# Linear attention and a highway layer: queries turned by VectorE, smaller products, pair stores, another order

## The chip, the cores and the metric

The kernel runs on one core of a Trainium2 chip. A core has five engines with a queue of instructions each: TensorE (PE in the profile; PEld are its weight loads), VectorE (DVE), ScalarE (ACT), GpSimd (POOL) and SyncE (SP), which here only issues DMAs. Sixteen DMA engines move data between HBM and SBUF. The metric is the device time of one execution, in microseconds, as the median of several runs: 118.83 us before the change (118.77 to 118.89 in three runs).

## The reference

Eight batches, eight heads, 576 tokens, 64 numbers a head. Attention without a score matrix, and behind it a highway layer with two 512x512 weights:

```
q_s = softmax of q over the 64 numbers of a token
k_s = softmax of k over the 576 tokens
kv  = k_s^T v                # 64x64 for each batch and head
x   = q_s kv                 # 4608 tokens of 512 numbers
H   = max(x w_h, 0)
T   = sigmoid(x w_t + b_t)
out = T H + (1 - T) x
```

Inputs and output are float32, 9.4 MB each for q, k, v and the output.

## The kernel before

The kernel is one long list of steps, ORDER, written out by hand; each engine takes its own steps in that order, and waits where a step needs another's result. A step's name tells its work and place: `kv_3_0` is batch 3, `mt_12_0` tile 12; a letter behind a colon picks the engine (A ScalarE, D VectorE, P GpSimd, F a whole step instead of halves).

Tokens are worked in 36 tiles of 128 rows: of each pair of batches four tiles come from the first, four from the second, and one holds the 64 last rows of both. Tiles 27 to 35 belong to batches 6 and 7.

For a batch, q, k and v are loaded with 64 partitions a head, two heads side by side (`load_kv` L183, `load_q` L199 to L206; batches 4 to 7 have another cut of q, in pieces of 1 KB and 256 B). ScalarE takes exp of k and q to float16 (`ek` L253, `eq` L298 to L307), `vc` (L259) casts v. `kv` (L269) multiplies keys and values in blocks of 64x64 with a column of ones behind v, which gives the sums; `kr` and `kn` (L281, L287) divide, into `kvb`, which holds two heads on a diagonal of blocks. TensorE transposes exp q (`qt` L319, L324) into PSUM, and VectorE or ScalarE copies it out (`qc` L333); batch 7 is turned by two DMA transposes instead (`qd` L340). `xu` (L361) is the product of queries and kv of a tile in four products of 130 columns, `rs` and `x` (L370, L376) divide by the sums of the queries.

Then the highway layer, per tile: four transposes of x (`xt` L384), copied out by `xe` (L391); a PSUM bank that is filled with the bias (`bw`: by ScalarE L399, or by a product L401), four products with w_t on top (`mt` L411), tanh (`th` L433, L435); four products with w_h (`mh` L419). The weights are prepared so that with w_h' = (w_h - 1)/2 the step `dd` (L439) gives d = max(x w_h', -x/2), `uu` u = (1 + tanh) d, and `oo` (L471) out = u + x. `uu` is either one VectorE operation that reads the gate from PSUM (L453) or, where ORDER says P, two GpSimd operations g and u (L450, L451). `st` (L479 to L491) stores.

PSUM has eight banks: two for gates (`ps_t`), two for w_h products (`ps_g`), two for kv and xu (`ps_x`, one buffer of two banks), one for turned queries, one for turned x. All loads and nearly all stores go through SP's one DMA queue, in ORDER's order. At the start, TensorE multiplies blanks (`fill` L167) until there is work; batches 0 and 1 and tiles 0, 4 and 5 are worked in halves.

Of the kernel before, what the change touches and what calls it, by code (L numbers as in the profile page):

```python
# [8 lines left out]
FP32 = mybir.dt.float32  # L9
FP16 = mybir.dt.float16  # L10
# [6 lines left out]
b_0 q_0_0 v_0_1 setupdve k_0_0 b_32 eq_0_0 bsplit setuppool fill_5 fill_8 bp v_0_0 bc qt_0_0 ek_0_1 v_0_3 ek_0_0 k_0_2  # L17
v_0_2 vc_0_3:A bw_1 vc_0_0 ek_0_2 vc_0_2 q_0_4 vc_0_1:D ek_0_3 bw_0 w_h_0 fill_8 qc_0_0 whd_1:P kv_0_0 eq_0_1 w_h_2
w_t_2 kr_0_0 whd_0:P whd_2:P w_t_0 k_1_2 v_1_2 q_1_0 k_1_0 v_1_0 fill_5 q_1_4 kn_0_0 q_2_0 k_2_0 eq_0_2 xu_0_0 v_2_0
q_3_0 rs_0_0 whc_0:A x_0_0 k_3_0 fill_4 v_3_0 kv_0_1 fill_3 kr_0_1 kn_0_1 xu_0_1 rs_0_1 xu_1_0 rs_1_0 qt_0_1 x_1_0  # L20
fill_6 whd_3:P qc_0_1 xt_1_0 xu_3_0 qt_0_2 qc_0_2:A xe_1_0:D fill_1 rs_3_0 x_3_0 x_0_1 xt_3_0 xu_2_0 rs_2_0 x_2_0
wtc_2:P whc_2:A mh_1_0 wtc_0:P vc_1_3 ek_1_3 ek_1_2 vc_1_0 xe_3_0:D mh_3_0 dd_1 xt_0_1 xt_0_0 mt_1_0 xe_0_0:D mh_0_0
xe_0_1 dd_3 xt_2_0 mh_0_1 mt_0_1 th_1_0 xe_2_0:D dd_0 vc_1_2:A kv_1_1 uu_1_0 oo_1_0 eq_1_0 mt_0_0 th_0_0 ek_1_0 ek_1_1
kr_1_1 bw_3 qt_1_0 vc_1_1:A kn_1_1 qc_1_0 mt_3_0 xu_5_1 uu_0_0 mh_2_0 th_3_0 bw_2 rs_5_1 x_5_1 dd_2 xu_4_1 kv_1_0
kr_1_0 eq_1_1 rs_4_1 xt_5_1 mt_2_0 th_2_0 kn_1_0 bw_5 xe_5_1:D x_4_1 xu_5_0 mt_5_1 qt_1_1 eq_1_2 rs_5_0 x_5_0 xt_5_0
xu_4_0 bw_4:A uu_3_0:P oo_3_0 xe_5_0:D mh_5_1 rs_4_0 x_4_0 mh_5_0 xt_4_1 qc_1_1:A xt_4_0 xe_4_1:D dd_5 eq_2_0 xe_4_0:D
v_4_0 mt_5_0 th_5_0 xu_6_0 qt_1_2 rs_6_0 qc_1_2 oo_0_0 mt_4_1 mh_4_1 mh_4_0 uu_2_0:P x_6_0 mt_4_0 eq_2_1 xt_6_0 xu_8_0
uu_5_0 bw_6:A xe_6_0:D qt_2_0 rs_8_0 x_8_0 mh_6_0 oo_5_0 th_4_0 xt_8_0 dd_4 uu_4_0 xu_7_0 mt_6_0 ek_2_0:F rs_7_0
vc_2_2:A bw_8 xe_8_0:D mt_8_0 x_7_0 th_6_0 xt_7_0 th_8_0 oo_2_0 vc_2_0 kv_2_0 oo_4_0 qc_2_0 q_4_0 bw_7:A qt_2_1
qc_2_1:A dd_6 uu_6_0:P oo_6_0 eq_3_0:F xe_7_0:D kr_2_0 kn_2_0 mh_8_0 xu_9_0 rs_9_0 x_9_0 mt_7_0 th_7_0 bw_9 dd_8  # L30
uu_8_0:P qt_2_2 qc_2_2:A xu_10_0 bw_10:A xt_9_0 xe_9_0:D rs_10_0 x_10_0 ek_3_0 mh_7_0 dd_7 ek_3_2 mh_9_0 xu_12_0 k_4_0
xt_10_0 k_5_0 rs_12_0 qt_3_0 xe_10_0:D x_12_0 mt_9_0 th_9_0 uu_7_0:P q_4_9 dd_9 xu_11_0 qc_3_0 vc_3_2:A xt_12_0
mt_10_0 rs_11_0 mh_10_0 x_11_0 v_5_0 q_5_0 vc_3_0 st_1_1 q_5_9 uu_9_0 dd_10 oo_7_0 kv_3_0 qt_3_1 th_10_0 oo_8_0 st_1_0
xe_12_0 bw_12:A mh_12_0 kr_3_0 qc_3_1:A kn_3_0 xu_14_0 rs_14_0 x_14_0 bw_11:A xt_11_0 xe_11_0 mt_12_0 th_12_0 qt_3_2
v_6_0 xt_14_0 oo_9_0 k_6_0 xu_13_0 q_6_0 xe_14_0 mh_11_0 dd_12 qc_3_2 mt_11_0 rs_13_0 eq_4_0:F th_11_0 uu_12_0
uu_10_0:P x_13_0 dd_11 xu_15_0 rs_15_0 vc_4_0 mh_14_0 x_15_0 st_5_1 dd_14 qt_4_0 oo_10_0 vc_4_2 xu_16_0 rs_16_0 x_16_0
xt_13_0 xe_13_0:D oo_12_0 bw_14:A bw_13:A ek_4_0:F st_3_0 mt_14_0 th_14_0 xu_17_0 rs_17_0 bw_15:A x_17_0 qc_4_0
xt_15_0 mt_13_0 kv_4_0 xe_15_0:D kr_4_0 uu_11_0:P oo_11_0 th_13_0 qt_4_1 uu_14_0:P st_3_1 mh_13_0 vc_5_2 xt_16_0
kn_4_0 mh_15_0 xe_16_0:D vc_5_0 xu_18_0 ek_5_0:F dd_13 xt_17_0 qc_4_1:A uu_13_0 xe_17_0:D dd_15 rs_18_0 oo_14_0
bw_16:A mt_15_0 mh_16_0 x_18_0 th_15_0 uu_15_0:P mt_16_0 dd_16 mh_17_0 oo_13_0 bw_17:A th_16_0 oo_15_0 kv_5_0 uu_16_0  # L40
kr_5_0 kn_5_0 oo_16_0 eq_4_2 dd_17 qt_4_2 xt_18_0 eq_5_0 mt_17_0 st_5_0 xe_18_0 xu_20_0 rs_20_0 mh_18_0 qc_4_2:A
bw_18:A q_7_0 th_17_0 mt_18_0 eq_5_1 bw_20:A uu_17_0:P x_20_0 xt_20_0 dd_18 vc_6_2 xe_20_0:D xu_21_0 th_18_0 rs_21_0
st_7_0 v_7_0 qt_5_1 qc_5_1:A mt_20_0 x_21_0 xt_21_0 uu_18_0 eq_5_2 xu_19_0 xe_21_0:D qt_5_0 rs_19_0 x_19_0 st_7_1
mh_20_0 qc_5_0 bw_21:A st_10_1 vc_6_0 mt_21_0 th_20_0 dd_20 ek_6_0:F xu_22_0 bw_19:A rs_22_0 x_22_0 qt_5_2 th_21_0
qc_5_2:A eq_6_0 mh_21_0 bw_22:A xt_19_0 xe_19_0:D kv_6_0 dd_21 kr_6_0 kn_6_0 xt_22_0 uu_20_0:P mh_19_0 mt_19_0
xe_22_0:D dd_19 oo_17_0 xu_23_0 rs_23_0 oo_20_0 oo_18_0 mt_22_0 eq_6_1 qt_6_0 th_19_0 x_23_0 xu_24_0 uu_19_0 th_22_0
xt_23_0 xe_23_0:D k_7_0 mh_22_0 rs_24_0 bw_23:A x_24_0 mt_23_0 qc_6_0 xu_25_0 rs_25_0 x_25_0 st_10_0 uu_21_0:P oo_19_0
# [10 lines left out]
mh_32_0 dd_33 th_33_0 uu_33_0 xu_35_0 bw_32:A rs_35_0 oo_33_0 xt_34_0 mt_32_0 bw_34:A xe_34_0:D mh_34_0 st_33_0 x_35_0  # L58
xt_35_0 mt_34_0 dd_32 th_32_0 bw_35_1 oo_30_0 st_16_0 st_30_0 uu_32_0 xe_35_0 oo_32_0 mh_35_0 th_34_0 bw_35_0 mt_35_0
th_35_0 mt_35_1 dd_34 uu_34_0 oo_34_0 dd_35 uu_35_0 st_32_0 th_35_1 uu_35_1 st_34_0 oo_35_0 st_35_0 oo_35_1:D  # L60
st_35_1:A
"""


# [469 lines left out]
```

## Time and profile before

| | |
|---|---|
| median of the runs | 118.83 us |
| span of the profiled execution | 116.9 us |
| what lies around the span, to the median | 1.9 us |
| instructions | 3424 |
| DMA packets, bytes | 24195, 40.58 MB |
| packets under 512 B, under 2 KB | 5362, 11762 |
| share of the 16 DMA engines taken by SP's queue | 96.9% |

How to read it: the busy line gives the time in which each engine worked and its share of the span; the slices cut the span in 40 equal parts of 2.9 us, a digit 9 is a slice that is busy for 90% or more. The chain that ended last is followed back from the last instruction. A group's line gives source line, engine, operation, output and inputs by name, shape, count, then busy time and mean duration, then the idle time ahead of it and who ended it. A line of the timeline begins with start and duration in microseconds.

### The profile page before, as it was taken

What the parts mean: (1) busy time and instruction counts of PE and PEld (TensorE: products, weight loads), DVE (VectorE), ACT (ScalarE), POOL (GpSimd) and SP (SyncE); (2) the same over time, 40 slices, a digit from 0 to 9 for tenths busy, and PEclk for the clock granted to TensorE, in tenths of its full rate; (3) what the DMA queues carried; (4) which work ended last, traced back from release to release, by engine and by line L of the source; (5) the groups of instructions that cost most, each with busy time, mean ns of one, the idle gap of its engine ahead of it and who ended that gap; (6) DMA issues with size and microseconds to landing.
All of it is one profiled execution on the core that took longest, in us unless ns stands there. A gap on an engine that the chain in (4) does not pass through costs nothing.

```text
span 116.9 us, 3424 instructions
## 1 busy us (share of the span) xinstructions
PE 109.5 (94%) x1351; PEld 61.6 (53%) x1351; DVE 93.3 (80%) x222; ACT 90.0 (77%) x132; POOL 89.1 (76%) x99
## 2 busy tenths in 40 slices
PE   5999987999999999999999999999999999999930
PEld 2354544545665656565665547566564555554520
DVE  5642587589799979979889798988989887899870
ACT  4356461897999999989999999998597998545520
POOL 5022237208996999999999999999989699999960
PEclk9999999999999999999999999999999999999998
DMA  2999999999999999999999999999999956992875
GB/s 42 399 392 377 408 398 385 375 377 379 393 391 397 383 391 393 358 375 387 357 376 360 387 392 363 390 381 383 399 398 217 302 204 270 397 404 115 315 295 179
DMA packets 24195, 40.58 MB, mean 347 GB/s; under 512 B 5362, under 2 KB 11762, under 8 KB 24180
## 3 DMA queue, kind: packets, MB, share of 16 engines
q1 hardware_dynamic: 24032, 40.24, 96.9%
q8 instruction: 10, 0.16, 0.6%
q10 hardware_dynamic: 148, 0.14, 0.4%
q14 instruction: 5, 0.04, 0.1%
HBM read 30.41 MB, written 9.44 MB: 341 GB/s over the span
## 4 chain that ended last, share of the span: by engine, by line
PE 67%; POOL 15%; issue 6%; DVE 5%; DMA 3%; SPq 1%; POOLq 0%; DVEq 0%
PE tps L411 18%; PE gps L419 16%; PE turned L167 9%; POOL o L471 7%; PE xu L361 6%; PE turned L384 5%; PE kv L269 5%; PE qps L324 4%; POOL u L451 4%; DMA out_dram<-o 3%; POOL g L450 2%; PE qps L319 2%; POOL v L259 2%; DVE x L376 2%; PE tps L401 1%
## 5 line engine op out<-in xcount | busy, mean ns | idle before, releaser
L471 POOL TENSOR_TENSOR o<-u,x 128x512 f32<-128x512 f16 (+1 forms) x36 | 40.6, 1143 | 1.6 <-DVE u L453 0.7
L411 PE MATMUL tps<-w16t,xT 128*128 128x512 f16 (+1 forms) x148 | 37.3, 373 | 0.0
L419 PE MATMUL gps<-w16h,xT 128*128 128x512 f16 x144 | 36.8, 379 | 0.5 <-DVE xT L391 0.5
L376 DVE TENSOR_TENSOR x<-xu,rs 128x512 f16<-128x512 f32 (+1 forms) x39 | 25.2, 649 | 2.4
L259 POOL CAST v<-v 128x1152 f16<-128x1152 f32 (+1 forms) x14 | 14.0, 1010 | 14.7 <-DMA v<-in_v_dram 13.7
L439 DVE SCALAR_TENSOR_TENSOR d<-x,gps 128x512 f16<-128x512 f16 x36 | 24.5, 680 | 0.3
L451 POOL TENSOR_TENSOR u<-g,d 128x512 f16<-128x512 f16 x17 | 19.7, 1158 | 1.7 <-DVE rs L370 0.4
L253 ACT ACTIVATE ek<-k 128x576 f16<-128x576 f32 (+2 forms) x15 | 17.9, 1225 | 3.0 <-DMA k<-in_k_dram 3.0
L419 PEld LDWEIGHTS <-xT 128*128 128x128 f16 x144 | 13.0, 98 | 12.3 <-DVE xT L391 1.8
L399 ACT COPY tps<-ball 128x512 f32<-128x512 f32 x28 | 16.6, 597 | 3.5 <-DVE u L453 3.2
L411 PEld LDWEIGHTS <-xT 128*128 128x128 f16 x148 | 13.2, 98 | 10.6 <-DVE xT L391 0.4
L361 PE MATMUL xu<-kvb,eq 128*128 128x130 f16 (+1 forms) x160 | 14.8, 224 | 0.2 <-DVE kvb L287 0.2
L384 PE MATMUL turned<-idh,x 128*128 128x128 f16 x144 | 14.2, 220 | 0.5 <-DVE x L376 0.5
L391 DVE COPY xT<-turned 128x512 f16<-128x512 f16 (+1 forms) x28 | 10.9, 391 | 4.2 <-PE turned L384 3.0
L435 ACT ACTIVATE tps<-tps 128x512 f32<-128x512 f32 (+1 forms) x20 | 11.2, 559 | 3.6 <-PE tps L411 3.3
L453 DVE SCALAR_TENSOR_TENSOR u<-tps,d 128x512 f16<-128x512 f32 (+1 forms) x19 | 12.7, 671 | 1.4 <-ACT tps L435 0.6
L361 PEld LDWEIGHTS <-eq 128*128 128x128 f16 (+1 forms) x160 | 10.0, 100 | 7.3 <-DVE x L376 2.5
L167 PE MATMUL turned<-blank 128*128 128x512 f16 x40 | 12.4, 458 | 1.5 <-POOL blank L149 1.3
L384 PEld LDWEIGHTS <-x 128*128 128x128 f16 x144 | 9.8, 98 | 6.0 <-DVE x L376 2.1
L307 ACT ACTIVATE qe<-q 128x1024 f16<-128x1024 f32 (+3 forms) x9 | 9.4, 1052 | 4.1 <-DMA q<-in_q_dram 4.1
L450 POOL TENSOR_SCALAR g<-th 128x512 f16<-128x512 f16 x17 | 10.6, 621 | 0.9 <-ACT th L433 0.9
L433 ACT ACTIVATE th<-tps 128x512 f16<-128x512 f32 x17 | 10.0, 594 | 0.9 <-PE tps L411 0.9
(48 smaller groups left out, 106.8 us busy)
## 6 DMA issues: line engine op xcount, KB each, us to landing
k<-in_k_dram SPq DMA_DIRECT2D x6, 1152.0 KB, 12.2
v<-in_v_dram SPq DMA_DIRECT2D x6, 1152.0 KB, 12.0
out_dram<-o SPq DMA_DIRECT2D x23, 256.0 KB, 4.0
q<-in_q_dram SPq DMA_DIRECT2D x10, 512.0 KB, 11.5
out_dram<-o SPq DMA_DIRECT2D x6, 512.0 KB, 3.8
k<-in_k_dram SPq DMA_DIRECT2D x4, 576.0 KB, 9.3
q<-in_q_dram SPq DMA_DIRECT2D x2, 1152.0 KB, 14.2
q<-in_q_dram SPq DMA_DIRECT2D x2, 640.0 KB, 10.5
```

What stands on the lines that cost most here:

```text
L167: nc.tensor.matmul(spare, blank[:, 0:P], blank, start=True, stop=True, skip_group_check=True)
L253: nc.scalar.activation(t[:, :, c:c + n].rearrange("p j c d -> p c j d"), T[f"k32{b}"][:, c:c + n].rearrange("p c (j d) -> p c j d", j=NJ), ...
L259: copy(v16[b % NV][:, c:c + n, :, 0:D], T[f"v32{b}"][:, c:c + n].rearrange("p c (j d) -> p c j d", j=NJ))
L361: nc.tensor.matmul(dst, turned_q(b, jp, n), kvb[b % NKV][:, hh, kk], start=True, stop=True, skip_group_check=True)
L376: nc.vector.tensor_mul(t[:, k0:k1], sums(i, k)[:, :, :, 0:64], T[f"rs{i}_{k}"][:, 0:k1 - k0].unsqueeze(3).to_broadcast([P, k1 - k0, 4, D]))
L384: nc.tensor.matmul(t[:, n], T[f"x{i}"][:, n0 + n % 2:n0 + 2 * P:2], idh, is_transpose=True, start=True, stop=True, skip_group_check=True)
L399: nc.scalar.copy(t[:, cs], ball[:, cs])
L411: nc.tensor.matmul(T[gate(i, k)][:, cs], T[f"xT{i}"][:, n], w16["t"][:, n, cs], start=False, stop=(n == parts[-1] and not first), skip_gro ...
L419: nc.tensor.matmul(t, T[f"xT{i}"][:, n], w16["h"][:, n], start=(first and n == parts[0]), stop=(n == parts[-1] and not (first and len(part ...
L439: nc.vector.scalar_tensor_tensor(t, T[f"x{i}"], -0.5, T[f"gps{i}"], op0=ALU.mult, op1=ALU.max)
L451: nc.gpsimd.tensor_mul(t, g, T[f"d{i}"])
L471: eng.tensor_add(t[:, cs], T[f"u{i}_{h}"][:, cs], T[f"x{i}"][:, cs])
```

## The change

Queries are loaded with 32 partitions a head, four heads side by side, in runs of 18 tokens (`load_q`). Their exponentials are turned by VectorE in blocks of 32x32 words of 32 bits, that is two float16 numbers at a time (`tr`), straight from SBUF to SBUF, in three pieces for a batch; `qt`, `qc` and `qd` are gone. Even and odd numbers of a head then lie two bytes apart, and so kv is computed in parts for even and for odd numbers: 64 rows, 32 columns of the output (`kv`, 144 products a batch). `xu` multiplies 32 rows by 65 columns with four heads in the four row parts of the array, each with a PSUM bank of its own, for two tiles at a time ("a group"; there are 20). `rs` and `x` work on a group at once. `ps_x` is now four banks, used by kv and xu in turn; gates and w_h products share three banks (`ps_g`).

`uu` is always two operations, g and u, and each of them, like o, is on VectorE or on GpSimd as ORDER says. Bias is copied by ScalarE in all tiles but the last. Nothing is halved at the start; only the last tile is. Stores are of two tiles, with 4 KB a row, but for five single ones. The weight casts are on VectorE but for one. Pools change their numbers of buffers, and ORDER is new altogether.

```diff
-    ps_t = pool("ps_t", 2, space=PS)
-    ps_g = pool("ps_g", 2, space=PS)
     ps_x = pool("ps_x", 1, space=PS)
-    ps_q = pool("ps_q", 1, space=PS)
+    ps_g = pool("ps_g", 3, space=PS)
     ps_xt = pool("ps_xt", 1, space=PS)
...
+    def load_q(e, b, j, n):
+        t = landing("q", b, ldq).rearrange("p (c f) -> p c f", c=2)
+        rows = q[b].rearrange("(c g) (p j) d -> (g p) c (j d)", g=4, p=NQ)
+        nc.sync.dma_start(t[:, :, j * D:(j + n) * D], rows[:, :, j * D:(j + n) * D])
...
+    def kv(e, b):
+        ps = T[f"kvps{b}"] = ps_x.tile([P, 4, DM], FP32, tag="xu", name=f"kv_{b}")
+        for turn in range(2):
+            for c in range(2):
+                for j in range(NJ):
+                    for g in range(4):
+                        h = 4 * c + g
+                        hh, i, m = h % 2, h // 2, (turn + h) % 2
+                        rows, cols = slice(64 * hh, 64 * hh + 64), slice(32 * g, 32 * g + 32)
+                        nc.tensor.matmul(
+                            ps[cols, m, 65 * c:65 * c + 65], T[f"ek{b}"][rows, j, i, m:D:2],
+                            v16[b % NV][rows, i, j, 0:65], start=(j == 0), stop=(j == NJ - 1),
+                            skip_group_check=True, tile_position=(64 * hh, 32 * g))
...
+    def tr(e, b, j, n):
+        t = once(f"et{b}", lambda: etp.tile([P, 2, NQ * NT, 2], FP16, tag="et", name=f"et_{b}"))
+        src = T[f"qe{b}"].rearrange("p c f -> p (c f)").bitcast(FP32).rearrange("p (c j d) -> p c j d", c=2, d=NQ)
+        dst = t.rearrange("p c n m -> p (c n m)").bitcast(FP32).rearrange("p (c n) -> p c n", c=2)
+        if n == 8:
+            dst = dst[:, :, NQ * j:NQ * j + 256].rearrange("p c (a t i) -> p c i a t", a=2, i=4)
+            src = src[:, :, j:j + n].rearrange("p c (i a) d -> p c i a d", a=2)
+        else:
+            dst = dst[:, :, NQ * j:].rearrange("p c (t i) -> p c i t", i=2)
+            src = src[:, :, j:j + n]
+        nc.vector.transpose(dst, src)
...
+    def xu(e, u):
+        bs, J, its = groups[u]
+        t = T[f"xu{u}"] = ps_x.tile([P, 4, DM], FP32, tag="xu", name=f"xu_{u}")
+        if len(bs) == 1:
+            for a in range(2):
+                for c in range(2):
+                    for m in range(2):
+                        for g in range(4):
+                            col = 65 * (2 * a + c)
+                            rows = slice(32 * g, 32 * g + 32)
+                            nc.tensor.matmul(
+                                t[:, g, col:col + 65], turned_q(bs[0], c, m, 256 * J + P * a, P)(rows),
+                                kvb[bs[0] % NKV][rows, m, c, 0:65], start=(m == 0), stop=(m == 1),
+                                skip_group_check=True, tile_position=(32 * g, 0))
+            return
...
+    def gg(e, i, h=0):
+        eng = nc.vector if e == "D" else nc.gpsimd
+        eng.tensor_scalar(t[:, cs], T[f"th{i}_{h}"][:, cs], 1.0, 1.0, op0=ALU.add, op1=ALU.mult)
+
+    def uu(e, i, h=0):
+        eng = nc.vector if e == "D" else nc.gpsimd
+        eng.tensor_mul(t[:, cs], T[f"g{i}_{h}"][:, cs], T[f"d{i}"][:, cs])
...
+    def st(e, u):
+        dst = rows_at(bs[0] * S + 8 * J, [[NT * DM, NQ], [2 * DM, 4], [1, 2 * DM]])
+        nc.sync.dma_start(dst, T[f"oo{u}"].rearrange("p a n -> p (a n)"))
```

The new order ends so:

```
... st_6 mh_25 dd_25 mh_24 xt_27 xe_27:D dd_24 oo_23_0:D eq_7_0_8
tr_7_0_8 xu_16 rs_16 k_7_0_4 x_16 th_25_0 gg_25_0:P ... ek_7_0_4 kv_7 th_27_0 gg_27_0:D ...
mt_35_0 th_35_0 dd_35 gg_35_0:D uu_35_0:D
oo_35_0:P mt_35_1 th_35_1 gg_35_1:D st1_35_0:A uu_35_1:D oo_35_1:D st1_35_1:A
```

More of the change, by code (lines that the diff above doesn't have):

```diff
@@ L22 @@
[L22 to L26, printed above, removed]
@@ L112 @@
     NKV, NV = 3, 2
[L113 removed]
+    kvb = [consts.tile([P, 2, 2, 66], FP16, name=f"kvb{i}") for i in range(NKV)]
     v16 = [consts.tile([P, 4, NJ, 66], FP16, name=f"v16_{i}") for i in range(NV)]
```

439 lines of the change are left out of this document (159 added, 280 removed).

## The prediction

> **What bounds the kernel now.** I read the page's busy line and its slices first, then the chain that ended last, then the groups with their shapes kept apart, the timeline around the last keys, and the stretches of ten microseconds.
>
> ```profile
> PE 109.5 (94%) x1351; PEld 61.6 (53%) x1351; DVE 93.3 (80%) x222; ACT 90.0 (77%) x132; POOL 89.1 (76%) x99
> ...
> PE   5999987999999999999999999999999999999930
> ...
> DMA  2999999999999999999999999999999956992875
> GB/s 42 399 392 377 408 398 385 375 377 379 393 391 397 383 391 393 358 375 387 357 376 360 387 392 363 390 381 383 399 398 217 302 204 270 397 404 115 315 295 179
> ...
> HBM read 30.41 MB, written 9.44 MB: 341 GB/s over the span
> ...
> PE 67%; POOL 15%; issue 6%; DVE 5%; DMA 3%; SPq 1%; POOLq 0%; DVEq 0%
> ```
>
> TensorE is full from about 20 us to 111 us, and the DMA engines are full at some 385 GB/s until about 87 us. Both matter: TensorE sets the pace now, but no kernel can work on keys that have not landed. The groups give the prices (count, busy us, mean ns):
>
> ```profile
> L439 DVE SCALAR_TENSOR_TENSOR d<-x,gps 128x512 f16<-128x512 f16 x36 | 24.5, 680 | 0.3
> L376 DVE TENSOR_TENSOR x<-xu,rs 128x512 f16<-128x512 f32 x33 | 22.8, 690 | 2.2
> ...
> L451 POOL TENSOR_TENSOR u<-g,d 128x512 f16<-128x512 f16 x17 | 19.7, 1158 | 1.7 <-DVE rs L370 0.4
> ...
> L391 DVE COPY xT<-turned 128x512 f16<-128x512 f16 x23 | 9.5, 413 | 2.7 <-PE turned L384 1.5 <-ACT tps L435 0.7
> ...
> L333 DVE COPY eq<-qps 128x1024 f16<-128x1024 f16 x8 | 5.5, 684 | 1.6 <-PE qps L324 1.6
> ...
> L376 DVE TENSOR_TENSOR x<-xu,rs 128x256 f16<-128x256 f32 x6 | 2.5, 423 | 0.2
> ```
>
> The timeline shows how the end hangs on the last batch: its keys become exponentials (L253) at 90.11, keys times values (L269) follows at 92.80, and the last product with the gate weights (L411) ends at 112.1.
>
> ```profile
> 90.11 2.12 ACT L253 ACTIVATE ek<-k 128x2304 f16<-128x2304 f32 x1
> ...
> 92.80 0.78 PE L269 MATMUL kv<-v,ek 64*64 64x65 f16 x72
> ...
> 111.05 1.04 PE L411 MATMUL tps<-w16t,xT 128*128 128x256 f16 x8
> ```
>
> Between 93.6 and 112.1 TensorE has 18.5 us, and the instructions behind that kv add up to 18.6 us: no idle time. From 112.1 to the end are 4.8 us of tanh, u, o and the last store.
>
> **The change, part by part.** I work against the profiled execution: span 116.9 us; the median of 118.83 lies 1.9 us above it, added at the end. TensorE prices are those of the chain of waits: 0.86 us for four 512-column products, 0.22 for four transposes of x, 0.45 for eight of q, 0.23 for one tile's xu, 0.71 to 0.78 for a kv of 72.
>
> TensorE. Gone: 128 transposes of q (16 x 0.45 = 7.1), seven bias products (1.5). kv: 8 x 144 small products instead of 8 x 72. They are again 65 columns, four beside each other on different parts of the array, so I take the measured 0.75/72 = 10.4 ns each: 1.5 us a batch, 6 us more in all. xu: 640 products of 32 rows and 65 columns instead of 128 + 32 of 130 columns. Ends: 10.4 ns (the kv row) or, with no overlap, half of the 57 ns that one xu product of 130 columns takes, 28 ns; 6.7 to 18 us against 8.4 now. The kv row is the nearest (same columns, partial array): 6.7, and 11 us more at the other end. After a kv the chain has 0.55 instead of 0.45 for the next eight transposes, so 0.1 us for a switch; there are 28 such blocks instead of 14: 1.4 more. Sum: -7.1 - 1.5 + 6 - 1.7 + 1.4 = -3 us of some 95.
>
> ScalarE. Without the q copies (6 x 1.01 + 6 x 0.38) but with seven more bias copies (0.6 each), and the exponentials of q whole: 90.0 becomes about 89. GpSimd: 15 of the o additions leave (1.16 each), three g come (0.62): 89.1 becomes about 74.
>
> VectorE. Gone: the q copies (6.0), the fused u that read PSUM (19, 12.7), the half-array kvb products (20, 7.4; now 8 x 0.424 = 3.4). x and its reciprocal go in pairs: 1024 elements are 0.690 + 2 x 0.267 = 1.22 (0.267 from the 256- and 512-element rows), 16 x 1.22 + 4 x 0.69 = 22.3 against 25.3. Added: 15 o of the 512 form (0.69, as x): 10. The 32x32 transposes (16 of 512 words, 8 of 128) have no row: between 0.35 (the 512-element cast, L236) and 1.22 (if the strided writes cost double); I take 0.62, between twice the 256-word memset (0.272) and the 0.68 of 512-element operations: 11.5 in all. 17 g: 0.35 to 0.69, taken 0.38 (nearest: the cast and the xT copy, one 16-bit source): 6. 20 u: 0.41 to 0.69, taken 0.5: 10. Weight casts and subtractions from POOL and ACT: 3. The groups now add to 101.5 us of durations for 93.3 busy (back to back, operations overlap: x at 47.67, u at 48.28, d at 48.88), mine to about 112, so 103 busy: 10 more. At the low ends it would be 6 us less, at the high ends 16 more.
>
> The new u, g and o on VectorE read only SBUF, while GpSimd reads SBUF for its own u, g and o. In the trace of before VectorE's elementwise work always has one operand in PSUM, and GpSimd's o never strays from 1.156 us (0.667 is the half tile), so a collision is not seen there, nor excluded. The bounds for one are 0 and one GpSimd operation (1.16).
>
> [...]
>
> DMA. The reads stay; q now comes in runs of 4.6 KB instead of 1 KB and 256 B, and the two DMA transposes go. What counts is when the last keys land, since all is in one queue. Before, ten stores of 262 KB stand in front of them: 30.4 - 0.26 + 2.6 = 32.8 MB, at 384 GB/s from 2.9 us on, 88 us; ScalarE took them at 90.1 without waiting. After, seven pair stores and two single ones stand in front: 34.6 MB. At 389 GB/s (slices 2 to 13, without the small q pieces) that is 2.9 + 34.5/0.389 = 91.6, and 0.7 for the landing (0.524 MB of q should be through at 3.9 and was taken at 4.68): 92.3. With 400 throughout (slices with 4 KB weight rows show 398 to 408) it is 89.9; with 380, 94.4. These nine stores wait for o of old tiles, which are long done, and loads are issued some 12 us ahead, so SP's queue should not starve.
>
> The start: batch 0 is no longer halved, so kv 0 needs all keys and values (2.4 MB: 9.5 us) but q comes after. The last w_h block lands at about 18, its subtraction and cast on VectorE take 1.5; the first products start at 17 to 20, as now (18.1). Nothing gained or lost: from 25 us the next keys set the pace.
>
> Middle. Counted with the rows, each VectorE duration less the 0.08 that overlaps, VectorE has 15.7 us queued between kv 5 and kv 6, TensorE 14. By the same rate kv 5 can start at 69.0 (24.65 MB through at 66.0, 0.7 to land, two casts of 1.15), kv 6 at 81.9 (29.8 MB, 0.7, exponential 2.1): 12.9 us. From kv 6 to kv 7 there are 10.2 us of TensorE work for 12.4. At full speed kv 7 is 0.6 late. Also gates and values now share three PSUM banks instead of two and two, and kv and xu one set of four, so each kv or xu waits for a 1.2 us x; the wait "xu for x" is 2.5 us in 8 cases now. At 95% of full speed the two stretches take 27.3 for 25.3: 2 us late.
>
> The end. Keys 92.3, exponential 2.1, kv 1.5: 95.9. Behind it TensorE has 8 tiles: 15 groups of four at 0.86 and two half ones (0.9), six transposes (1.3), three xu (1.0), switches (0.4): 16.6. Then 4.85 as now, with g and u (0.8) in place of a 0.42 u partly beside other work. 95.9 + 16.6 + 4.85 = 117.3 without any stall. The late middle adds 2; VectorE has 16 us of work in the same 16.6, so I add 0.8 for waits (xu of the last group waits for a pair's x with 1.9 us of products to cover 2.4). 120.1; plus 1.9: **122.0 us**, slower by 2.7%. Undisturbed, 119.2; at 389 GB/s and 90% of full speed, 124.5.
>
> **The rivals.** *Faster.* The DMA runs at 400 GB/s with the longer runs: keys at 89.9, and both VectorE and TensorE keep their tail full. 89.9 + 2.1 + 1.5 + 16.6 + 4.85 + 1.9 = 116.9; it decides once keys land before 91.6 us and nothing stalls. For it: the kernel before has a tail without idle time. Against it: VectorE had 20% of slack there and has none here.
>
> *VectorE and GpSimd get in each other's way.* Some 53 VectorE operations read SBUF alone; GpSimd is busy 74 of 118 us (0.63), the rest of an operation is half of 1.16: 0.37 us each on average. 27 of the 53 stand in the two stretches where VectorE has no slack (8 after kv 5, 19 after kv 7): 10 us, of which I take 4 to fall into the slack before kv 7 or behind GpSimd's last work: 122 + 6 = 128 us. For it: nothing before put both engines on SBUF together. [...]
>
> *The small products don't overlap.* xu costs 28 ns: 0.56 us more for each of 20 groups; four groups after kv 5 and three after kv 7 are on the path: 122 + 4 = 126. Against it: the kv row.
>
> **How the numbers follow.** Forecast (119.3 to 124.5): 0.45. Collision (124.5 to 131): 0.27. Small products: 0.07. Faster: 0.17, and within 0.2%, which is about what a measurement of this kernel can tell from no change: 0.04. Range 117.0 to 128.8: it leaves out some of the faster cases and the upper half of the collisions, 2 in 10. Faster 0.17, same 0.04, slower 0.79.
>
> **What would show it.** kv 7 near 96 to 98 us with the exponential in front waiting for the DMA; VectorE at 100 busy us or more; xu at 0.33 us a pair in the chain; transposes near 0.62; tail of some 22 us from kv 7 on. It is wrong if VectorE's g, u and o run far longer than 0.38, 0.5 and 0.69 beside GpSimd, if small products do not overlap, or if the keys land before 91.6.

## The result, and the profile after

The changed kernel takes 145.87 us, 27.0 us more than the kernel before, which took 118.86 us beside it: a ratio of 1.2258, with a 95% interval of 1.222 to 1.2296. One of its four executions fell into a slower state and took 152.99 us; executions over 1.5% above the fastest of their kernel count in the median of 145.87, but in no ratio, and in no time of the experiments below, where the changed kernel stands at 145.7 us. The prediction was 122.0 us with a range of 117.0 to 128.8. Slower was right; the size was not, by 24 us, and none of the rivals reached so far: the collision with GpSimd, the dearest of them, was put at 131 us at most. The profiled execution took 145.68 us with a span of 143.6.

The page of the changed kernel, with the lines that answer to those of the kernel before, and the line of the queue that fetches instructions:

```profile
PE 109.4 (76%) x2266; PEld 56.9 (40%) x2266; DVE 114.4 (80%) x216; ACT 83.3 (58%) x112; POOL 76.3 (53%) x82
...
PE   6965097597697798578799745999985999799430
...
PEclk9999658999999999999999996899999999999997
DMA  4999999999999799996599940795991280813233
GB/s 144 355 385 411 399 391 389 391 399 402 388 403 375 246 376 409 379 395 266 167 349 383 383 159 6 230 407 201 304 306 62 112 335 0 322 48 146 108 145 114
...
q8 instruction: 17, 0.28, 0.8%
...
HBM read 30.41 MB, written 9.44 MB: 277 GB/s over the span
...
DVE 47%; PE 30%; issue 8%; DMA 7%; SPq 3%; POOL 1%; ACT 1%; DVEq 0%; POOLq 0%
```

TensorE's busy time is what it was (109.5 before), but spread over 27 us more, with 24 of the 40 slices under 90% (5 before), and twice within the kernel its clock falls. The DMA engines are no longer full: 277 GB/s for 341. VectorE has 21 us more work than before, and leads the chain. "issue", time for which the profile names no releaser, is 8% of a longer span. The costliest groups of VectorE, and its g, shapes kept apart:

```profile
L363 DVE SCALAR_TENSOR_TENSOR d<-x,gps 128x512 f16<-128x512 f16 x36 | 24.0, 676 | 2.0 <-PE gps L353 2.0
L320 DVE TENSOR_TENSOR x<-xu,rs 128x1024 f16<-128x1024 f32 x16 | 19.5, 1220 | 0.8
L279 DVE STREAM_TRANSPOSE et<-qe 128x512 f32<-128x512 f32 x16 | 17.5, 1103 | 4.8 <-ACT qe L261 4.8
L375 DVE TENSOR_TENSOR u<-g,d 128x512 f16<-128x512 f16 x18 | 12.1, 676 | 0.9
L387 DVE TENSOR_TENSOR o<-u,x 128x512 f32<-128x512 f16 x14 | 11.1, 796 | 0.8 <-POOL u L375 0.7
...
L369 DVE TENSOR_SCALAR g<-th 128x512 f16<-128x512 f16 x15 | 7.1, 474 | 0.0
```

What the new work costs is higher than I took it: the turn 1.10 us for 0.62, u 0.68 for 0.5, o 0.80 for 0.69, g 0.47 for 0.38. The x of a pair is 1.22, as forecast.

The end, from the timeline (start, duration): the last exponentials of keys, the last keys times values, the last gate product, the last o of VectorE.

```profile
113.18 2.12 ACT L223 ACTIVATE ek<-k 128x2304 f16<-128x2304 f32 x1
...
115.77 1.35 PE L244 MATMUL kv<-v,ek 64*32 64x65 f16 x144
...
136.70 1.03 PE L347 MATMUL tps<-w16t,xT 128*128 128x256 f16 x8
...
139.86 0.43 DVE L387 TENSOR_TENSOR o<-u,x 128x256 f32<-128x256 f16 x1
```

kv 7 starts at 115.8 instead of 92.8; from there to the end of the span it is 27.8 us instead of 24.1. So 23 of the 27 us are lost before the last batch.

**Where TensorE stops.** The timeline of TensorE around the second dip of its clock:

```profile
83.44 1.44 PE L244 MATMUL kv<-v,ek 64*32 64x65 f16 x137 [0.75 <-DVE x L320]
87.66 0.29 PE L244 MATMUL kv<-v,ek 64*32 64x65 f16 x7 [2.79 <-issue]
87.88 0.61 PE L327 MATMUL turned<-idh,x 128*128 128x128 f16 x4
88.28 1.91 PE L353 MATMUL gps<-w16h,xT 128*128 128x512 f16 x4
```

In the middle of one kv, 137 of 144 products done, TensorE stands still for 2.8 us though keys and values are there, and nothing on another engine ends the wait. Afterwards four products take 1.91 us instead of 1.03, and the granted clock is 0.50 from 87.31 to 90.72. A stop of 2.6 us of the same kind lies within an xu and ends at 61.85. The records of the instruction queue (16 KB blocks) show a block that comes in from 59.29 to 60.38 and one from 84.81 to 86.23; TensorE goes on 1.47 and 1.43 us after these. That was not in the prediction, and the experiments are mostly about it.

### The profile page after: what moved, and what is told of

Its sections match the earlier page's. It is cut to its first block, busy times and chain, and to the rows that moved or that the text cites. A ratio compares the mean times of both kernels' runs of the same rounds, so it can differ in the third digit from the quotient of the medians.

```text
span 143.6 us, 5179 instructions
## 1 busy us (share of the span) xinstructions
PE 109.4 (76%) x2266; PEld 56.9 (40%) x2266; DVE 114.4 (80%) x216; ACT 83.3 (58%) x112; POOL 76.3 (53%) x82
## 4 chain that ended last, share of the span: by engine, by line
DVE 47%; PE 30%; issue 8%; DMA 7%; SPq 3%; POOL 1%; ACT 1%; DVEq 0%; POOLq 0%
PE gps L353 11%; DVE x L320 8%; DVE d L363 7%; DMA q<-in_q_dram 7%; PE tps L347 6%; DVE o L387 6%; DVE et L279 6%; DVE u L375 6%; PE turned L327 4%; PE kv L244 4%; DVE xT L333 4%; DVE g L369 3%; PE xu L292 3%; SPq L169 2%; DVE w16h L199 2%
## 5 line engine op out<-in xcount | busy, mean ns | idle before, releaser
L359 ACT ACTIVATE th<-tps 128x512 f16<-128x512 f32 (+1 forms) x37 | 21.1, 580 | 27.2 <-PE tps L347 27.1
L387 POOL TENSOR_TENSOR o<-u,x 128x512 f32<-128x512 f16 (+1 forms) x22 | 25.1, 1139 | 19.4 <-DVE u L375 18.6
L279 DVE STREAM_TRANSPOSE et<-qe 128x512 f32<-128x512 f32 (+1 forms) x24 | 19.9, 834 | 4.8 <-ACT qe L261 4.8
L320 DVE TENSOR_TENSOR x<-xu,rs 128x1024 f16<-128x1024 f32 (+1 forms) x20 | 22.3, 1114 | 0.8
L261 ACT ACTIVATE qe<-q 128x1024 f16<-128x1024 f32 (+1 forms) x16 | 18.6, 1161 | 7.2 <-DVE et L279 4.4
L369 POOL TENSOR_SCALAR g<-th 128x512 f16<-128x512 f16 x20 | 14.2, 717 | 15.6 <-ACT th L359 15.6
L223 ACT ACTIVATE ek<-k 128x2304 f16<-128x2304 f32 (+1 forms) x10 | 17.3, 1735 | 4.0 <-DMA k<-in_k_dram 4.0
L244 PE MATMUL kv<-v,ek 64*32 64x65 f16 x1152 | 11.8, 192 | 5.6 <-issue 3.2
L375 DVE TENSOR_TENSOR u<-g,d 128x512 f16<-128x512 f16 (+1 forms) x20 | 13.0, 655 | 1.1
L244 PEld LDWEIGHTS <-ek 64*32 64x32 f16 x1152 | 10.4, 91 | 8.5 <-issue 5.0
L333 DVE COPY xT<-turned 128x512 f16<-128x512 f16 x27 | 11.0, 408 | 2.2 <-PE turned L327 2.0
```

What stands on the lines that cost most here:

```text
L244: nc.tensor.matmul(ps[cols, m, 65 * c:65 * c + 65], T[f"ek{b}"][rows, j, i, m:D:2], v16[b % NV][rows, i, j, 0:65], start=(j == 0), stop=(j ...
L261: nc.scalar.activation(t[:, :, j * D:(j + n) * D], src[:, :, j * D:(j + n) * D], AF.Exp)
L279: nc.vector.transpose(dst, src)
L320: nc.vector.tensor_mul(dst[:, :, 0:n], sums(u)[:, :, :, 0:64], T[f"rs{u}"][:, :, 0:n].unsqueeze(3).to_broadcast([P, 4, n, D]))
L359: nc.scalar.activation(t[:, cs], T[f"tps{i}_{h}"][:, cs], AF.Tanh, scale=0.5)
L375: eng.tensor_mul(t[:, cs], T[f"g{i}_{h}"][:, cs], T[f"d{i}"][:, cs])
```

## The experiments

Two theories. *VectorE*: its work, 93 to 114 us, and the lengthening beside GpSimd set the pace. *Instructions*: the 144 products of a kv, each with a weight load, use up TensorE's instructions faster than they arrive; it stops, and its clock falls. Either would leave the late transfers as a consequence. All times are medians beside the kernel before (118.8 to 119.0). Where the time rests on one execution, the text says "single": two executions of one of these kernels can lie 2 to 5 us apart, so that a single one decides only about more.

### One part at a time

**e1_plain_turn**: the turned blocks are written side by side (the rows of x then stand in another order).

```diff
-dst[:, :, NQ * j:NQ * j + 256].rearrange("p c (a t i) -> p c i a t", a=2, i=4)
+dst[:, :, NQ * j:NQ * j + 256].rearrange("p c (i a t) -> p c i a t", a=2, i=4)
```

> The 32x32 blocks are written next to each other instead of four words apart (the numbers of x land at other tokens; the amount of work is the same). Before the change a 512-element operation took 0.68 us; the turn of 512 words takes 1.10 us in the changed kernel. If the strided write doubles it, it falls to about 0.6, VectorE is 8 us shorter and the time falls by 6 to 9 us from 145.9. If a turn simply costs two cycles for each word, it stays at 1.10 and the time stays within 1 us.

149.5 us, single. The turn alone, from the groups of this run:

```profile
L279 DVE STREAM_TRANSPOSE et<-qe 128x512 f32<-128x512 f32 x16 | 11.0, 694 | 4.8 <-ACT qe L261 4.8
```

So 0.41 of the 1.10 us are the strided write, and without it the turn is near the 0.62 that I took. VectorE's busy time falls by 5.6 us, to 108.8, and the time does not fall, which neither expectation had. TensorE has three long stops for instructions here (2.06, 4.92 and 2.12 us) instead of two.

**e2_no_pool_gu**: GpSimd's g and u left out.

```diff
 def gg(e, i, h=0):
+    if e != "D":
+        T[f"g{i}_{h}"] = T[f"th{i}_{h}"]   # and u likewise: d
+        return
```

> All g and u that ORDER gives to GpSimd are left out (20 and 17 operations, 36 us of GpSimd; u then takes tanh or d in their place, so the output lacks these factors); those on VectorE stay. Theory of the collision: VectorE's g falls from a mean of 0.47 towards 0.28 and its u from 0.68 towards 0.42, the values that they have in the changed kernel when GpSimd rests; VectorE gets 5 to 8 us shorter and the time falls by 5 to 9 us. Rival, that these are the operations' own durations: means stay, and the time falls by less than 3 us, by the shorter way from tanh to o alone.

150.7 us, single. VectorE's g falls to 0.42, u to 0.62 in the eight that still read a g (0.50 in the ten others), o to 0.77, and its busy time by 2.5 us, less than the 5 to 8 expected. The time does not fall; the stops are 2.06, 5.63 and 2.73 us.

**e3_kv64**: kv in 72 products of 64x64, as before the change.

```diff
-ps[cols, m, 65 * c:65 * c + 65], T[f"ek{b}"][rows, j, i, m:D:2],
+ps[cols, hh, 65 * c:65 * c + 65], T[f"ek{b}"][rows, j, 2 * c + w],   # 64 columns
```

> Keys times values in 72 products of 64x64 a batch as before the change, instead of 144 of 64x32 (the blocks then lie where the queries don't look for them, so x is another one; reads, waits and the rest of the order stay). 1152 instructions fewer in TensorE's queue. Theory of the instruction supply: the blocks of instructions on the queue for them fall from 17 to about 12, the two waits of 2.6 and 2.8 us of TensorE that end with no other engine named go, and with 5 us less of products the time falls by 5 to 10 us. Rival, VectorE is full anyway: the gain becomes idle time of TensorE, and the time falls by less than 2 us.

141.38 us, single; VectorE leads the chain with 57%, its busy time is unchanged at 113.7, 13 instruction blocks come in instead of 17, and there is no stop over 1 us for instructions. A gain of 4.3 us, with TensorE 3 us less busy; it lies between the two expectations and within what two executions can differ by.

**e4_act_stores**: every store on ScalarE's queue.

```diff
-nc.sync.dma_start(dst, T[f"oo{u}"].rearrange("p a n -> p (a n)"))
+nc.scalar.dma_start(dst, T[f"oo{u}"].rearrange("p a n -> p (a n)"))
```

> All stores are issued by ScalarE's queue, at the same places of the order, so that loads behind them in SP's queue don't wait for them. In the changed kernel the keys of batch 7 are issued at 99.7 us, behind stores that wait for o. Theory of the queue: they are issued before 85 us, kv 7 comes 8 us earlier or more and the time falls by 5 to 10 us. Rival, that VectorE's and TensorE's work sets the pace and the late loads are only its consequence: the keys come earlier, kv 7 does not, and the time moves by less than 2 us, or up a little for the waits on ScalarE.

149.76 us, single; the keys of batch 7 leave at 73.0, but kv 7 starts at 117.9, no earlier. Nothing that I did to one part alone was worth more than 4.3 us, and what was to help VectorE helped nothing. Either of two causes could stand behind the other, so the next runs put each into the kernel before, alone.

### Each cause alone, in the kernel before

**e5_before_kv32** and **e9_before_kv32_look** (the same kernel): each 64x64 product becomes two of 64x32.

```diff
+for s in (0, 32):
-    nc.tensor.matmul(ps[cols, ...], T[f"ek{b}"][rows, j, 2 * kk + w], ...)
+    nc.tensor.matmul(ps[64 * w + s:64 * w + s + 32, ...], T[f"ek{b}"][rows, j, 2 * kk + w, s:s + 32], ...)
```

> The kernel before with one thing changed: each 64x64 product of keys times values is made of two products of 64x32 that write the same sums, 576 more pairs of TensorE instructions (about the number of the changed kernel), everything else as it was, VectorE's work too. Instruction supply as a cause of its own: waits of 2 us or more inside or right before kv that nothing on another engine ends, an instruction block landing where they end, a granted clock of 0.5 behind them, and 126 to 138 us. VectorE as the only cause: the dearer kv alone, 8 x 0.75 = 6 us on a TensorE that is 94% busy, no such waits, 123 to 125 us.

> The same kernel as e5_before_kv32 once more, for a profile that is not disturbed. Instruction supply: 142 to 146 us again; waits of 1 us or more on TensorE put down to nothing on another engine (issue) in or right before kv, each ending when a 16 KB instruction block lands, and stretches of granted clock 0.5 behind them; VectorE some 94 busy us as before. If kv itself is what takes the 25 us: keys times values of 3 us and more each without gaps, clock 1.0.

143.91 us (ratio 1.2096, 1.2061 to 1.2132), and 143.76 in e9, single: 25 us more, above the 126 to 138 of the first expectation, with VectorE's work unchanged at 93.7 busy us. One more execution of e5, the one that was profiled, took 228 us (so did one of the kernel before beside it, 224) and tells nothing of the time. TensorE's waits, its granted clock in 40 slices, and the timeline around the first stop, all of e9:

```profile
PE kv L270 <- issue: 10.0, 3, 5.0
PE gps L422 <- issue: 4.5, 1, 4.5
...
PEclk9999999999999998699975799996599999999998
```

```profile
49.81 1.21 PE L270 MATMUL kv<-v,ek 64*32 64x65 f16 x127
56.06 0.32 PE L270 MATMUL kv<-v,ek 64*32 64x65 f16 x17 [5.04 <-issue]
56.31 1.04 PE L327 MATMUL qps<-idh,qe 128*128 128x128 f16 x8
57.14 1.91 PE L422 MATMUL gps<-w16h,xT 128*128 128x512 f16 x4
```

Three stops of 5.04, 4.46 and 4.67 us, 14.2 in all, where the kernel before has none. With each the granted clock falls to 0.5, together for 17 us; 13.2 of them lie behind the stops, which at half speed are worth up to 6.6 us. A kv itself takes 1.35 to 1.47 us where no stop falls in it.

**e10_before_kv130**: the 72 products stay, each 130 columns wide.

```diff
-ps[cols, hh, 65 * kk:65 * kk + 65], ..., v16[b % NV][rows, 2 * kk + w, j, 0:65],
+ps[cols, hh, 130 * kk:130 * kk + 130], ..., v16[...][rows, ..., 0:65].unsqueeze(1).to_broadcast([64, 2, 65]),
```

> The kernel before with each of the 72 products of keys times values 130 columns wide instead of 65 (the values twice beside each other; the second half is not read): TensorE's time for keys times values doubles by about as much as in e5_before_kv32 (0.75 us a batch, 6 us in all), the number of instructions stays. If the number of instructions cost e5_before_kv32 its 25 us: 122 to 126 us, no waits for instructions, clock near 1.0. If it was TensorE's time or PSUM: 135 to 145 us, as e5_before_kv32.

122.34 us (1.0253 to 1.033), as expected if the number of instructions was the cause.

```profile
PE 113.1 (94%) x1351; PEld 64.9 (54%) x1351; DVE 93.5 (78%) x222; ACT 90.1 (75%) x132; POOL 88.9 (74%) x99
```

A kv of six batches takes 1.26 us for 0.78, so TensorE has nearly the extra work of e9 (there 1.35 to 1.47), no instruction more, no stop and no dip of the clock. It costs 3.5 us. The other 21 us of e9, less some 0.1 to 0.2 us a kv, come with the number of instructions; the stops and the half clock behind them, 14.2 and up to 6.6 us, account for nearly all of it.

**e16_before_turns**: two turns a batch on VectorE, written as the changed kernel writes them, into a tile that nothing reads.

```diff
 def kn(e, b, k):
+    for s in range(2):
+        nc.vector.transpose(aside.rearrange("p (c a t i) -> p c i a t", c=2, a=2, i=4), words_of_ek[512 * s ...])
```

> The kernel before with two turns of 512 words a batch added on VectorE behind the normalized keys times values, with the same strided writes as the changed kernel's, into a tile that nothing reads: 16 x 1.10 = 17.6 us more VectorE work, 111 of 117 us busy, no TensorE instruction more. The counterpart of e9_before_kv32_look. If VectorE's work alone can cost the old kernel its 27 us: 126 to 140 us. If VectorE's slack takes most of it: 119 to 124 us.

134.44 us (ratio 1.131, 1.1245 to 1.1376), within the 126 to 140 for VectorE's work alone.

```profile
L294 DVE STREAM_TRANSPOSE aside<-ek 128x512 f32<-128x512 f32 x16 | 17.8, 1114 | 1.7 <-ACT ek L253 1.2
```

17.8 us more VectorE work cost 15.6 us, although VectorE idled 24 of 117 us before. Its slack was not usable for these: they stand in pairs of 2.2 us behind a kv, ahead of the x and the copies of turned queries that TensorE waits for next. The place counts, then, as well as the amount. Either cause alone can therefore cost the old kernel a lot: the instructions 21 to 25 us, the turns put in this place 16.

### Both in the changed kernel

**e6_kv64_plain_turn**: e3 and e1 together.

> The changed kernel with keys times values as 72 products of 64x64 (as in e3_kv64, so sums land in other places) and with the turned blocks written side by side (as in e1_plain_turn; the rows of x then stand in another order). Compared with e3_kv64 (141.4 us) it differs by the turns alone, and there are no long instruction waits to hide what they are worth. If VectorE sets the time once instructions arrive: 16 turns are 0.41 us shorter each, 6.5 us of busy time, and most of it shows: 135 to 138 us, last keys times values before 109 us. If the time hangs on instruction supply or transfers: 140 to 142 us, as e3_kv64.

136.29 us (ratio 1.1434, 1.1351 to 1.1517), as expected if VectorE sets the time once instructions arrive. With 72 products the shorter turn is worth 5 us (against e3, single); with 144 (e1) it was worth nothing.

**e13_no_turn** and **e14_kv64_no_turn**: the turns of batches 1 to 7 left out, with 144 products and with 72.

```diff
 def tr(e, b, j, n):
+    if b > 0:
+        T[f"et{b}"] = T["et0"]
+        return
```

> The changed kernel with the turns of batches 1 to 7 left out (the query weights of batch 0 are used for all batches): VectorE is some 16 us less busy, TensorE's instructions are the 2266 pairs of the changed kernel. If instruction supply holds the changed kernel by itself: 142 to 151 us, no gain against 145.9. If VectorE's work sets the time: 128 to 134 us.

> e13_no_turn with keys times values as 72 products of 64x64: 1152 TensorE instructions fewer, the same VectorE work. Compared with e3_kv64 (141.4 us) it differs by the turns, compared with e13_no_turn by the instructions. If both causes hold, either hidden behind the other: 122 to 130 us, 10 us or more under e3_kv64 and 12 us or more under e13_no_turn. If VectorE's work is not a cause: 134 to 141 us, as e6_kv64_plain_turn and e11_kv64_plain_fused.

146.23 us (145.7 to 147.1) and 132.44 us (131.9 and 133.0). The busy lines, e13 and then e14:

```profile
PE 112.6 (78%) x2266; PEld 58.8 (41%) x2266; DVE 101.2 (70%) x195; ACT 83.1 (57%) x112; POOL 76.8 (53%) x82
```

```profile
PE 101.5 (78%) x1690; PEld 52.0 (40%) x1690; DVE 101.1 (78%) x195; ACT 82.6 (63%) x112; POOL 78.0 (60%) x82
```

With 13 us less VectorE work the 144 products hold the time where it was: four stops for instructions, 9.7 us for the 5.4 of the changed kernel, and a granted clock of 0.5 for 14 us in the middle. Only with 72 products does the work taken from VectorE show. e14 fell between its two expectations: 14 us under e13, but 9 us under e3 where 10 or more were expected. Without the turns xu no longer waits for the exponentials of its queries either, and that is in these two times.

**e11_kv64_plain_fused** and **e12_plain_fused**: VectorE's pairs of g and u are one operation on PSUM again, with 72 and with 144 products.

```diff
+nc.vector.scalar_tensor_tensor(u, T[f"tps{i}_{h}"], 1.0, T[f"d{i}"], op0=ALU.add, op1=ALU.mult)
-g = th + 1; u = g * d
```

> e6_kv64_plain_turn (136.5 us) with one step less than e8_kv64_plain_fused_back: where g and u are both VectorE's they are one operation on the tanh in PSUM again, while the casts and subtractions of the gate weights stay on VectorE. Some 5 us less busy on VectorE, which was 97 to 99% busy from 40 us on in e6_kv64_plain_turn. If VectorE sets the time there: 130 to 133.5 us, and the 139 us of e8_kv64_plain_fused_back come from its start. If VectorE's busy time does not matter: 136 to 139 us.

> e11_kv64_plain_fused with keys times values in 144 products of 64x32 as in the changed kernel, so the changed kernel with turned blocks side by side and with g and u fused on VectorE. VectorE is some 11 us less busy than in the changed kernel. If instruction supply is a bound of its own there: 141 to 149 us, hardly below the 145.9 of the changed kernel, waits for instructions of 2 us and more, and 8 us or more above e11_kv64_plain_fused. If VectorE alone sets the time: 132 to 137 us, within 4 us of e11_kv64_plain_fused.

137.75 us (1.1561 to 1.1646) and 150.06 us (1.2536 to 1.2711). In e11 the second expectation came true: VectorE is only 2 us less busy (107.1, for the 5 that I took) and the time rises a little. The gate stays in PSUM until the fused operation has read it, and the wait of ScalarE's next bias copy for VectorE's d, 9.3 us in e6, is 16.3 here. The gap between the two, 12.3 us, is the price of the 144 products once more: their stops, the half clock behind these, and some 5 us of TensorE's own work.

**e8_kv64_plain_fused_back**: e11, and the weight casts and subtractions back on GpSimd and ScalarE (six letters in ORDER, such as `wtc_2:D` to `wtc_2:P`).

> e6_kv64_plain_turn with VectorE's load taken down to about that of before: where g and u are both VectorE's they are one operation on the tanh in PSUM again, as before the change, and the casts and subtractions of the gate weights go back to GpSimd and ScalarE. VectorE overfull as the main cause of what is left: some 8 us less busy, the first product with the gate weights earlier than 24 us, 125 to 131 us. Something else (the order of the work, the wider exponentials, PSUM shared by kv, xu and x): VectorE's busy time falls, but the time stays at 133 us or more.

139.08 us (1.1636 to 1.1725); here too the second expectation came true: VectorE 102.5 busy, and no gain. Its busy time by itself is not the measure; at the start it only moves the wait (VectorE 3.5 of 10 us busy from 20 to 30 us, 7.8 in e6).

The square, in us; an asterisk marks a single execution:

```
                                  144 products   72 products   difference
turn as changed                      145.7          141.4*         4.3
turn side by side                    149.5*         136.3         13.2
turn side by side, g and u fused     150.1          137.8         12.3
no turns in batches 1 to 7           146.2          132.4         13.8
```

Down the left column nothing helps, down the right one the turns do. My reading: the instructions hold the left column near 146 or above, and in the changed kernel itself VectorE stands so close behind them that removing them alone shows 4.3 us. The square fits this; that the upper right corner is a single execution leaves the 4.3 uncertain by some us.

**e7_kv64_plain_no_pool_gu** and **e15_kv64_no_turn_no_pool_gu**: e6 and e14 without GpSimd's g and u.

> e6_kv64_plain_turn without GpSimd's g and u (left out: the steps behind them read the tanh and the difference instead). VectorE keeps every instruction. If VectorE loses time because its SBUF-only operations run beside GpSimd: g from about 0.47 to 0.35 us, u from 0.68 to 0.5, o a little shorter, some 5 us of VectorE's busy time, and 128 to 133 us (part of it because o no longer waits for GpSimd's u). If collisions are a side matter: VectorE's durations stay, and 134 to 138 us, within 1.5 us of e6_kv64_plain_turn.

> e14_kv64_no_turn without GpSimd's g and u. VectorE's instructions are the same, but fewer of them run beside GpSimd, and o waits less. If the lengthening beside GpSimd (some 5 us of VectorE's time in e7_kv64_plain_no_pool_gu against e6_kv64_plain_turn) is on the path: 2 to 5 us less than e14_kv64_no_turn. If VectorE has slack again without the turns: within 1.5 us of e14_kv64_no_turn.

131.51 us, single, with 133.6 to 135.4 in three further executions, and 130.45 us (ratio 1.0974, 1.0905 to 1.1042). In e15 that is 2.0 us less than e14; in e7 it is 4.8 less than e6, of which its own spread leaves 1 to 5. VectorE's g falls from 0.55 to 0.44 in both; its o (0.78 and 0.83 on average, 0.79 and 0.81 before) gets no shorter. GpSimd's own o and casts still run. The o's of VectorE also wait less for GpSimd's u, so that not all of the gain is lengthening.

**e17_late_stores** and **e18_no_turn_no_pool_gu_late_stores**: three stores behind the load of the last keys, in the changed kernel and in e15.

```diff
-... st1_17_0 ... st_10 st_6 ... k_7_0_4 ...
+... k_7_0_4 st1_17_0 st_10 st_6 ...
```

> The changed kernel with three stores (groups 10 and 6 and the half tile 17) placed in SP's queue behind the load of the last keys instead of ahead of it; nothing else. Where the stops of TensorE set the time, late loads are their consequence: the last keys are issued earlier than 99.7 us, but the time stays at 143 to 147 us. If the order of SP's queue holds the end by itself: keys some 8 us earlier and 137 to 141 us.

> e15_kv64_no_turn_no_pool_gu (130.5 us) with the same three stores behind the load of the last keys. There the last keys are issued at 88.7 us, 11 later than in the kernel before (77.7), behind stores that wait for o of groups that are not done. If with fewer stops and less VectorE work the order of SP's queue is the next limit: keys issued before 82 us, their exponential before 94 (99.45 in e15), and 124 to 128 us. If VectorE and TensorE could not use earlier keys: 129.5 to 131.5 us.

148.12 us (1.2412 to 1.2525) and 129.67 us (1.0844 to 1.0976). The keys of batch 7 are issued in e17 from 76.0 on, 24 us earlier than in the changed kernel, and its kv 7 starts at 118.1 for 115.8. In e18 they are issued at 72.4 and kv 7 starts at 102.2 for 101.6. e17 ends a little above the 143 to 147 expected for stops that set the time, so earlier keys gained nothing. Loads are late because the work is late; the expectation that the queue would be the next limit in e18 was wrong.

### All stops side by side

From the trace's records I counted TensorE's instructions (weight loads, products and its few semaphore instructions, in order of start) up to each stop, and looked up the instruction block that came in last. These are the stops of 1.1 us and more that the profile puts down to issue:

```
kernel   instructions before the stop     length, us               goes on after the block's end by, us
after    1985, 3009                       2.61, 2.79               1.47, 1.43
e9       1729, 2241, 3009                 5.04, 4.46, 4.67         1.58, 1.53, 1.36
e13      961, 1985, 2497, 3009            1.44, 1.64, 4.66, 2.00   1.58, 1.43, 1.29, 1.43
e12      1985, 2497, 3009                 2.03, 4.85, 1.79         1.39, 1.43, 1.43
e17      1985, 3009                       1.61, 4.75               1.41, 1.62
e14      2241                             2.10                     1.58
e15      2241                             2.71                     1.53
e18      2241                             2.71                     1.57
before, e3, e8, e10, e11, e16: none
```

All these counts leave 193 over when divided by 256, and so do those of e1, e2, e4, e5, e6 and e7: 29 stops in fourteen traces. My estimate from this remainder and from the blocks fetched (17 for 4545 instructions of TensorE in the changed kernel, 10 for 2716 in the kernel before; 4545 less 193 is 17 times 256) is 256 instructions to a block. 28 of the stops lie in a burst of small products, xu or kv; e9's second lies 0.8 us behind a kv. All end 1.3 to 1.6 us after a block has come in. A kv issues 288 instructions in 1.35 to 1.5 us; one block takes 0.9 to 1.9 us to come in. Why a block comes late, in e9 one that begins 2.3 us after TensorE has stopped, the traces do not show.

The kernel before and e10 have no such stop; e9, with two products for each one of a kv, stands still for 14.2 us in three. Nor does the clock fall behind every stop. In the changed kernel the granted clock is 0.50 from 87.31 to 90.72 us, behind the stop of 2.79 us, and stays at 1.00 behind that of 2.61. TensorE was busy for 0.98 of the 3.41 us ahead of that dip, and for 1.08 of the 3.42 us ahead of the other one, 15.63 to 22.45 us. The stop of 2.61 us lies in two stretches of 3.41 us, from 56.59 on, with 2.66 and 1.56 us of TensorE work. In e1 the clock is 0.8 and 0.6 in the two slices around the end of a stop of 2.06 us (59.1 to 66.5 us), and 0.9 or more behind one of 2.12 us that ends at 93.2. The length of a stop alone does not tell whether the clock falls.

## Why the prediction was wrong, and where it was right

**TensorE, "-3 us of some 95".** The prices were right: kv 1.35 to 1.5 us for 1.5 forecast, 10 ns a product; xu of a pair 0.35 to 0.36 us in the chain for 0.33; so the rival of small products that do not overlap is out. The step that failed is the sum itself: it counts what products cost and has no line for the instructions that carry them. 1.68 times as many (2266 pairs for 1351) come in bursts, and TensorE stops for them, 2.61 and 2.79 us in the changed kernel. In the kernel before this costs 21 us beyond TensorE's own work (e9 less e10). In the changed kernel taking the extra products away, with their own work, is worth 4.3 us alone (single) and 12 to 14 once VectorE has less to do.

**VectorE, "103 busy, 10 more".** It became 114.4, 21 more. The turn was mis-sized: 1.103 for 0.62, all turns together 19.9 us for 11.5, and 0.41 us of each of the 16 large ones is the strided write (e1); it lay inside the bounds of 0.35 to 1.22, and the reason given for the upper bound, strided writes, was the one that decided. g, u and o took 7.5, 13.0 and 11.5 us for 6, 10 and 10.

**The collision with GpSimd.** What this rival supposes is there. Near the end, VectorE and GpSimd in order of time:

```profile
132.63 0.43 DVE L375 TENSOR_TENSOR u<-g,d 128x512 f16<-128x512 f16 x1
132.98 0.29 DVE L369 TENSOR_SCALAR g<-th 128x512 f16<-128x512 f16 x1
133.14 1.15 POOL L387 TENSOR_TENSOR o<-u,x 128x512 f32<-128x512 f16 x1 [0.76 <-DVE u L375]
133.37 1.20 DVE L375 TENSOR_TENSOR u<-g,d 128x512 f16<-128x512 f16 x1
134.49 0.41 DVE L333 COPY xT<-turned 128x512 f16<-128x512 f16 x1
134.65 1.15 POOL L387 TENSOR_TENSOR o<-u,x 128x512 f32<-128x512 f16 x1 [0.36 <-DVE u L375]
134.83 1.12 DVE L369 TENSOR_SCALAR g<-th 128x512 f16<-128x512 f16 x1
```

A u takes 0.43 alone and 1.20 when GpSimd's o runs, a g 0.29 and 1.12; both end 0.15 to 0.28 us after that o. The copy from PSUM at 134.49 keeps its 0.41, and the o its 1.15. Over the whole trace, sorted by whether GpSimd worked at the same time (mean us):

```
        alone        beside GpSimd
g       0.28 (8)     0.70 (7, up to 1.12)
u       0.41 (8)     0.89 (10, up to 1.28)
o       0.68 (6)     0.89 (8, up to 1.60)
turn    1.07 (3)     1.11 (13)
d       0.68 (15)    0.68 (21)
```

The d reads PSUM. That is some 9 us of VectorE's time (7 x 0.41 + 10 x 0.48 + 8 x 0.21), and 0.37 us for each of 25 operations where I took 0.37 for each of 53: the size was right, the count was not. That an operation waits out the rest of GpSimd's was my assumption for the 0.37; no run shows it, only how much longer the operations took. What it is worth in time was tried only by halves: 2.0 us for GpSimd's g and u in e15, 1 to 5 in e7. A u has two SBUF inputs and a g one, and both take longer beside GpSimd, up to 1.28 and 1.12 us; a turn, with one, takes 1.11 us for 1.07. What decides, no run shows. (The prediction's "always" was not exact either: in the trace of before the cast of v, 0.75 us, and the subtraction that splits the bias work on SBUF alone; both ran too rarely to show a collision.)

**DMA, "SP's queue should not starve".** It did. The keys of batch 7 left SP's queue at 99.7, behind two stores that had waited:

```profile
90.45 0.49 SPq L169 DMA_DIRECT2D v<-in_v_dram  x1
98.43 1.20 SPq L396 DMA_DIRECT2D out_dram<-o  x2
99.72 0.74 SPq L169 DMA_DIRECT2D k<-in_k_dram  x1
```

"Nine stores wait for o of old tiles, which are long done" was true of the order and not of the clock: with the work 20 us late these o were not done. That the landing of the last keys sets the end, which the sum of 92.3 + 2.1 + 1.5 rests on, fell with e17 and e18: earlier keys did not shorten either kernel.

**The start, "nothing gained or lost".** Before and after, 10 to 30 us, TensorE's busy time in the third column (then weight loads, VectorE, ScalarE, GpSimd, the clock, DMA):

```profile
10.00:20.00 10.00, 8.71 (x131) 4.80 (x128) 6.97 (x20) 4.98 (x7) 4.47 (x7) 1.00 1.04 394
20.00:30.00 10.00, 10.00 (x136) 5.16 (x134) 7.83 (x22) 8.28 (x14) 4.07 (x6) 1.00 1.07 378
```

```profile
10.00:20.00 10.00, 4.37 (x149) 2.48 (x150) 3.90 (x7) 4.72 (x5) 0.46 (x1) 0.78 1.04 403
20.00:30.00 10.00, 7.45 (x67) 3.55 (x66) 8.83 (x15) 4.88 (x6) 4.29 (x4) 0.88 1.05 390
```

TensorE is 6.9 us less busy from 10 to 30 us, blanks counted in both, at a lower clock: q lands behind the keys, the first turn ends at 17.1, and TensorE waits 4.4 us for kvb, whose division stands behind that turn on VectorE; the weight work behind it lets the first product with w_h begin at 24.84 instead of 18.1. kv 1 starts at 31.1; its two halves did at 23.2 and 27.5.

**The end, 16.6 + 4.85 = 21.5 us from the end of kv 7.** It was 26.5 (143.6 less 117.1), because VectorE, 8.5 to 9.9 of every 10 us busy there, and not TensorE sets its pace. GpSimd at 76 us (forecast 74) was near. ScalarE has 83; the forecast was 89, though its own terms (8.3 us of copies less, 4.2 us of bias copies more) give 86.

**What stays open.** Without the extra products, the turns and GpSimd's g and u the changed kernel still takes 130.45 us, 11.6 more than before (e15). The start, one stop of 2.7 us with 3.4 us of half clock behind it, and the new order are in there; I did not take them apart. Nor do the products, the turn and the collision account for the whole miss: e7, with 72 products, a turn of 0.69 us and no g and u on GpSimd, is still 9.5 us above the 122.0 of the forecast.

## What to carry to other kernels

Cutting a product into smaller ones can add little to TensorE's work and still cost a fifth of the kernel (e9): count the instructions of a burst, look for "issue" in the middle of one, and for a granted clock of 0.5 behind it. When two causes stand behind each other, undoing one shows little; put each alone into the kernel before, and make a square of both. Work that goes to VectorE is to be priced with its write pattern (a turn 0.69 or 1.10 us) and with what GpSimd does at that moment (a g 0.28 or up to 1.12), not by its element count alone.

## What the runs showed that I had not expected

- TensorE stopped for instructions 29 times in fourteen traces, always at a count that leaves 193 when divided by 256, for 1.2 to 5.6 us, and went on 1.3 to 1.6 us after a block of 16 KB had come in.
- Nearly the same TensorE work cost the kernel before 3.5 us in 72 products a batch and 25 us in 144 (e10, e9).
- In the changed kernel the granted clock fell to 0.50 behind 3.4 us with 0.98 or 1.08 us of TensorE work, and stayed at 1.00 behind 3.41 us with 1.56; behind a stop of 2.06 us in e1 it fell, behind one of 2.61 us in the changed kernel it did not.
- A VectorE turn of 512 words in 32x32 blocks took 0.69 us when the words of a block were written side by side (e1) and 1.10 when they were written four words apart (changed kernel); of the latter, 1.07 alone and 1.11 beside GpSimd.
- VectorE's g, on SBUF alone, took 0.28 us by itself and up to 1.12 beside GpSimd, a u 0.41 and up to 1.28, while d, which reads PSUM, took 0.68 both ways.
